# Key-value sums built transposed in two-part features, with K's maxima as a bias of the exponentials and five weight blocks streamed through one buffer

## The chip, the cores and the metric

The kernel runs on one core of one Trainium2 chip. The metric is the device time of one execution in microseconds. A core has five engines that work at the same time and meet through semaphores: TensorE (PE, matmuls; its weight loads are shown as PEld), VectorE (DVE), ScalarE (ACT), GpSimd (POOL) and SyncE (SP), whose queue issues all DMA transfers of this kernel. Each engine works through its own instructions in order. Matmuls write to PSUM (8 banks of 128 x 512 float32), everything else lives in SBUF or, outside the core, in DRAM.

## The reference

For 8 batches and 8 heads of 576 rows and 64 columns, a linear attention with an exponential feature map is computed, and then a mixer with a low-rank token step and a two-layer channel step.

```python
def phi(x):
    proj = np.einsum('bhsd,df->bhsf', x, w_phi)            # d_feat = 128
    proj = proj - np.max(np.abs(proj), axis=-1, keepdims=True)
    return np.concatenate([np.exp(proj), np.exp(-proj)], axis=-1)
q_p, k_p = (phi(q), phi(k))
kv = np.einsum('bhsf,bhsd->bhfd', k_p, v)
z = np.sum(k_p, axis=2)
num = np.einsum('bhsf,bhfd->bhsd', q_p, kv)
den = np.einsum('bhsf,bhf->bhs', q_p, z)[..., None] + 1e-06
attn = num / den            # then heads side by side: x of 8 x 576 x 512
xt = x.transpose(0, 2, 1)
u = x + (xt @ U @ V).transpose(0, 2, 1)                    # rank 32 over the 576 rows
out = u + np.maximum(u @ w_ch1, 0.0) @ w_ch2               # 512 -> 2048 -> 512
```

So every feature vector of K and Q has 256 entries: the exponential of the shifted projection, and the exponential of its negative, where the shift is the largest absolute value of the row. w_ch1, w_ch2, U and V arrive as float64.

## The kernel before

**Attention.** The work unit is a pair of heads of one batch (class Pair; 32 pairs). Of the 576 rows, 512 are the main part (NT = 4 tiles of 128 rows) and 64 are the tail; the tails of both heads are worked on together. A pair goes through eight steps: s_project_k0, s_project_k1, s_project_q0, transposes (of the pair that comes next), s_kv0_q1, s_kv1, s_out0, s_out1. The main loop has the current pair cur at its outputs while the next pair nxt is projected and summed, and a third one, far, is loaded. project_k makes the projections of K for one head, k_features takes the row maxima (L348), subtracts them (L350) and makes both halves of the features with two exponentials over all four tiles (L353, L354). kv_tail and kv_main (L436, L443) multiply the features (f32, 128 x 128, stationary) with V (f32, 65 columns, moving) into one PSUM bank; the 65th column of V is all ones, so that it gives z. kv_done copies the bank to SBUF (L449), and out_tail and out_main (L469, L482) multiply Q's features with it; normalize divides.

**Two parts.** Float32 operands are multiplied in two ways. Tiles typed F32 go to PE as they are. Elsewhere a value is split into a high part, rounded to the type F32R, and a low part, the rest; products of these parts are accumulated. From batch 2 on (self.split, SPLIT = 2, 24 pairs) the projections of K and Q work in two parts, on data that was transposed by 32 x 32 blocks on DVE (L315) after a DMA that reads with 128-byte runs (L265).

**Mixer.** One group of 512 rows (class Mixer; nine groups: eight batches, and one made of all tails) goes through 16 blocks f of the hidden layer. hidden(f) makes 12 matmuls of 512 columns into ph (L619; one PSUM bank of its own), ACT and DVE take the rectified high and low parts out (L624, L625), and add(f) makes 12 matmuls into four banks o (L640). The order of a group's chunks is hidden(0), hidden(1), add(0), hidden(2), add(1) and so on. The chunks of a batch's group are dealt out over the steps of the next batch's attention, 28 of 32 over 34 steps, by Pace.step: after each attention step comes one chunk, or none.

**Weights.** w_ch1 and w_ch2 come as float64 words, are made float32 by convert on ACT, DVE and POOL, and split in two parts during the first batches, while mixer group 0 runs. All 16 blocks stay in SBUF (pool home, tags w1_f and w2_f) but for two: blocks 0 and 8 are stored to DRAM (kept) once, and from group 1 on they take turns in block 0's buffer (STREAM, function stream, L204): when the last matmul that reads one of them is issued, the load of the other is issued. Blocks 8 and 15 are kept in a buffer for both matrices at once (WHOLE); that of block 8 (w_late) later holds y, the group's rows that come in transposed (L605, L611).

**Order.** The program is written in one order, and a planner, which simulates the engines' times, arranges each engine's instructions from it; the order on each engine is then fixed. The PSUM banks are 3 of tag at (attention and token step), 1 of tag ph and 4 of tag o. Where tokens() and the mixer's first rows come at the end of a batch, the next pair's last four steps are dealt in between.

Of the kernel before, what the change touches and what calls it, by code (L numbers as in the profile page):

```python
# [21 lines left out]
P = 128  # L22
# [3 lines left out]
def tile_kernel(  # L26
# [160 lines left out]
    WHOLE = {LAST: "w_last", 8: "w_late"}  # L187
    STREAM = (0, 8)
    kept = {f: dram.tile([P, 2, 2, C], F32, name=f"kept{f}") for f in STREAM}

    def place(f, dt, shape, name):

        if f in WHOLE:
            both = home.tile([P, 2, *shape], dt, tag=WHOLE[f], name=name)
            return both[:, 0], both[:, 1]
        return [home.tile([P, *shape], dt, tag=f"w{n}_{f}", name=f"{name}_{n}") for n in (1, 2)]

    def stream(n, g, f):

        to = STREAM[1 - STREAM.index(f)]  # L200
        if g == 0 or g == B and to == 0:
            return
        w = home.tile([P, 2, C], F32R, tag=f"w{n + 1}_0", name=f"w{n + 1}_{to}_{g}")
        nc.sync.dma_start(out=f32(w), in_=kept[to][:, n])  # L204
        (w1_t, w2_t)[n][to] = w
# [9 lines left out]
    def convert_block(i):  # L215
        f, n = divmod(i, 2)
        r = convert(words[f][n], f"w{n + 1}_{f}")
        if f not in WHOLE:
            w = home.tile([P, 2, C], F32R, tag=f"w{n + 1}_{f}", name=f"w{n + 1}_{f}")
            split_w((nc.scalar.copy, nc.vector.tensor_copy)[n], r, w)  # L220
        elif n == 0:
            found[f] = r
            return
        else:
            w1_w, w = place(f, F32R, (2, C), f"w_{f}")
            split_w(nc.scalar.copy, found[f], w1_w)
            split_w(nc.vector.tensor_copy, r, w)
            w1_t[f] = w1_w
# [20 lines left out]
    class Pair:  # L249
# [93 lines left out]

        def k_features(self, n, k_w, kp):
# [4 lines left out]
                out=mk, in_=k_w, axis=AX.X, op=ALU.max, apply_absolute_value=True)  # L349
            nc.vector.tensor_tensor(  # L350
# [40 lines left out]
        def project_k_split(self, g):  # L391
# [13 lines left out]
            return self.k_features(g, k_w, kp)  # L405
# [26 lines left out]
        def kv_tail(self):  # L432
            self.kv_ps = self.ps("kv_ps", True)
            self.kv_v = self.kv_ps[:, 0:4 * (D + 1)].rearrange("p (f h e) -> p f h e", f=2, h=2)
            for f in range(2):
                nc.tensor.matmul(  # L436
                    self.kv_v[:, f, :, :], self.kpt[:, 0, f * F:(f + 1) * F], self.vt,
                    start=(f == 0), stop=False, skip_group_check=True)
# [59 lines left out]
        def s_project_k1(self):  # L498
            self.kp1 = self.project_k(1)
            self.project_q_tail()  # L500

        def s_project_q0(self):
            self.qp0 = self.project_q(0)

        def s_kv0_q1(self):
            self.kv_tail()
# [3 lines left out]
        def s_kv1(self):  # L510
            self.kv_main(1, self.kp1)
# [318 lines left out]
    if True:  # L830
# [17 lines left out]
        for n, (b, j) in enumerate(pairs):  # L848

            far = Pair(*pairs[n + 2]) if n + 2 < len(pairs) else None  # L850
# [84 lines left out]
```

## Time and profile before

| | |
|---|---|
| time, median of 3 runs | 1227.1 us (1226.07 to 1227.72) |
| the profiled execution: time, span | 1233.19 us, 1231.4 us |
| mean granted clock of TensorE | 0.992 |
| busy: PE, DVE, ACT, POOL | 1204.2, 690.9, 538.2, 203.6 us |
| DMA: bytes moved, mean busy share of q1 | 100.60 MB, 31.2% |

The span runs from the first to the last instruction of the profiled execution; a little of its time lies outside it. The busy time of an engine is the union of its instructions' times. Line numbers are those of the kernel before. A row of the groups gives line, engine, operation, the tile written and those read, shapes, the count, then busy time, the mean duration of one in ns, and the idle time of the engine ahead of them with what ended it. A row of a timeline gives the start, the time taken and what ran, with a count where equal ones follow each other. Durations of matmuls overlap, since they are pipelined.

### The profile page before, as it was taken

The numbers are of one execution on the slowest core, as the hardware profiler recorded it, in microseconds if no ns is written. First come the engines' busy times: TensorE is split into PE (matmuls) and PEld (weight loads), VectorE is DVE, ScalarE is ACT, GpSimd is POOL, SyncE is SP. The second block draws the span as 40 slices with busy tenths as digits, with TensorE's granted clock in tenths as the row PEclk, the third lists the DMA queues.
The fourth block names the chain that finished last, engine by engine and source line by source line (L and its number), as shares of the span: only waits on it lengthen the run. The fifth ranks groups of instructions, "written<-read, shape, count | busy, mean of one in ns | idle before, by whom it ended". The sixth has DMA issues, their size and how long they took to land.

```text
span 1231.4 us, 18285 instructions
## 1 busy us (share of the span) xinstructions
PE 1204.2 (98%) x6667; PEld 1036.6 (84%) x6669; DVE 690.9 (56%) x1517; ACT 538.2 (44%) x1151; POOL 203.6 (17%) x154
## 2 busy tenths in 40 slices
PE   8999998999999999999999999999999999999997
PEld 7887787888888888888888888888888888888886
DVE  5857879775566656665647556655656543312111
ACT  6866678554543444444534444344434431111110
POOL 3533444211110111011111111011201110000000
PEclk9979999999999999999999999999999999999999
DMA  4766221331234213431244123421343015400201
GB/s 133 241 227 208 70 64 30 90 109 25 54 97 116 48 40 91 90 99 30 64 115 111 28 52 86 111 69 26 88 107 98 1 52 150 112 35 1 69 1 35
DMA packets 248345, 100.60 MB, mean 82 GB/s; under 512 B 215360, under 2 KB 227904, under 8 KB 248256
## 3 DMA queue, kind: packets, MB, share of 16 engines
q1 hardware_dynamic: 248256, 99.44, 31.2%
q8 instruction: 53, 0.87, 0.3%
q14 instruction: 36, 0.29, 0.1%
HBM read 78.41 MB, written 20.97 MB: 81 GB/s over the span
## 4 chain that ended last, share of the span: by engine, by line
PE 78%; DVE 8%; SPq 4%; ACT 4%; DMA 4%; issue 1%; POOL 0%; DVEq 0%; ACTq 0%; POOLq 0%
PE ph L619 27%; PE o L640 27%; PE kv_ps L443 7%; PE xp L482 7%; SPq L605 2%; SPq L265 2%; PE pk L399 2%; DVE w L236 1%; PE pp L561 1%; PE kv_ps L436 1%; PE pq L422 1%; DMA raw<-in_q_dram 1%; PE pq L423 1%; PE xpt L469 1%; DMA y<-u_dram 1%
## 5 line engine op out<-in xcount | busy, mean ns | idle before, releaser
L619 PE MATMUL ph<-uT_hi,w 128*128 128x512 f32 x1152 | 389.0, 395 | 4.7 <-DVE h_lo L625 3.3
L640 PE MATMUL o<-w,h_hi 128*128 128x512 f32 x1152 | 327.1, 395 | 3.2 <-ACT h_hi L624 3.2
L619 PEld LDWEIGHTS ph<-uT_hi,w 128*128 128x128 f32 x1152 | 216.2, 188 | 51.2 <-DVE h_lo L625 5.6
L640 PEld LDWEIGHTS o<-w,h_hi 128*128 128x128 f32 x1152 | 211.1, 188 | 45.3 <-ACT h_hi L624 4.9
L619 PE MATMUL ph<-uT_lo,w 128*128 128x512 f32 x576 | 225.1, 391 | 0.0
L624 ACT ACTIVATE h_hi<-ph 128x512 fp32r<-128x512 f32 x144 | 85.9, 596 | 272.0 <-PE ph L619 261.0
L625 DVE SCALAR_TENSOR_TENSOR h_lo<-ph,h_hi 128x512 fp32r<-128x512 f32 x144 | 98.6, 685 | 176.6 <-ACT h_hi L624 175.4
L640 PE MATMUL o<-w,h_lo 128*128 128x512 f32 x576 | 191.9, 395 | 0.6 <-DVE h_lo L625 0.6
L363 POOL PARTITION_ALL_REDUCE qp<-qp x64 | 126.7, 1980 | 286.6 <-ACT qp L362 268.1
L443 PEld LDWEIGHTS kv_ps<-vb,kp 128*128 128x128 f32 x1024 | 126.6, 195 | 2.8
L482 PEld LDWEIGHTS xp<-kv,qp 128*128 128x128 f32 x1024 | 124.1, 194 | 4.8 <-DVE kp L403 0.9
L619 PEld LDWEIGHTS ph<-uT_lo,w 128*128 128x128 f32 x576 | 108.3, 188 | 21.3 <-DVE uT_lo L244 0.6
L443 PE MATMUL kv_ps<-vb,kp 128*128 128x65 f32 x1024 | 126.0, 274 | 0.1
L482 PE MATMUL xp<-kv,qp 128*128 128x65 f32 x1024 | 124.0, 274 | 0.6 <-DVE kp L403 0.6
L640 PEld LDWEIGHTS o<-w,h_lo 128*128 128x128 f32 x576 | 105.4, 188 | 21.6 <-DVE h_lo L625 1.3
L353 ACT ACTIVATE kp<-kp 128x512 f32<-128x512 f32 x64 | 40.4, 632 | 132.9 <-DVE kp L350 83.4
L363 POOL PARTITION_ALL_REDUCE qp_t<-qp_t x32 | 27.2, 851 | 403.2 <-ACT qp_t L362 401.0
L319 DVE TENSOR_TENSOR T<-raw,T 64x512 fp32r<-64x512 f32 x96 | 68.5, 714 | 33.6 <-ACT T L318 31.1
L315 DVE STREAM_TRANSPOSE raw<-raw 128x512 f32<-128x512 f32 x48 | 34.1, 711 | 80.3 <-DMA raw<-in_q_dram 36.8
L318 ACT CAST T<-raw 64x512 fp32r<-64x512 f32 x96 | 59.3, 618 | 33.9 <-PE pq L423 23.4
L365 ACT ACTIVATE qp<-qp 128x512 f32<-128x512 f32 x64 | 40.4, 631 | 59.8 <-DVE qp L364 59.5
L146 POOL INT64_ADD w_ab<-w_ab x32 | 44.1, 1377 | 76.0 <-DVE w_ab L142 40.4
(128 smaller groups left out, 1357.1 us busy)
## 6 DMA issues: line engine op xcount, KB each, us to landing
words<-in_moe_w_ch_dram SPq DMA_DIRECT2D x32, 512.0 KB, 8.0
w<-kept SPq DMA_DIRECT2D x30, 512.0 KB, 4.1
vb<-in_v_dram SPq DMA_DIRECT2D x64, 128.0 KB, 2.5
u_dram<-x SPq DMA_DIRECT2D x32, 256.0 KB, 2.2
st<-u_dram SPq DMA_DIRECT2D x16, 512.0 KB, 4.0
out_dram<-st SPq DMA_DIRECT2D x32, 256.0 KB, 2.3
y<-u_dram SPq DMA_DIRECT2D x112, 64.0 KB, 2.4
raw<-in_k_dram SPq DMA_DIRECT2D x192, 32.0 KB, 2.0
```

The source lines that it names most:

```text
L146: nc.gpsimd.int64_add(a64, a64, b64)
L318: nc.scalar.copy(out=m[here, s, :], in_=x_[here])
L319: nc.vector.tensor_sub(m[there, s, :], x_[here], f32(m[here, s, :]))
L353: nc.scalar.activation(out=kp[:, :, 0:F], in_=kp[:, :, F:2 * F], func=AF.Exp)
L363: nc.gpsimd.partition_all_reduce(qp[:, 0, :], qp[:, 1, :], P, ReduceOp.absmax)
L365: nc.scalar.activation(out=qp[:, 0, :], in_=qp[:, 1, :], func=AF.Exp)
L443: nc.tensor.matmul(self.kv_v[:, f, g, :], kp[:, t, f * F:(f + 1) * F], self.vb[:, g, t, :], start=False, stop=(t == NT - 1), skip_group_ch ...
L482: nc.tensor.matmul(xv[:, c, :], qp[:, f, c * P:(c + 1) * P], self.kv[:, f, c // 2 if self.split else s, :], start=(f == 0), stop=(f == 1))
L619: nc.tensor.matmul(ph, w1_part(f, l, c), r[:, c, :], start=(n == 0), stop=(n == 3 * NCC - 1))
L624: on_act = nc.scalar.activation(out=h_hi, in_=ph, func=AF.Relu)
L625: on_dve = nc.vector.scalar_tensor_tensor(out=h_lo, in0=ph, scalar=0.0, in1=f32(h_hi), op0=ALU.max, op1=ALU.subtract)
L640: nc.tensor.matmul(self.o[t], l[:, cs], w2_t[f][:, r, :], start=(f == 0 and n == 0), stop=(f == NFC - 1 and n == 2))
```

## The change

All of it is for the 24 pairs of batches 2 to 7, but for the weights' homes.

- The sums over the rows are built transposed. v_parts splits V in two parts that lie side by side (v_hl, 128 columns: 64 high, 64 low) and serve as the stationary operand; k_parts splits K's features in two parts (khi, klo), which move, 256 columns each. kv_turned makes 4 tiles x 2 parts = 8 matmuls a head in F32R, and the upper and lower half of the result are added to kvT (features in the free dimension). kv_end, called at the start of the iteration in which the pair is cur, turns kvT back with two f32 transposes, has kv_tail's matmuls in front of the sum, and adds the parts into kv.
- z of the main rows no longer comes from a column of ones: k_sums adds up the four tiles on DVE, sums over partitions on POOL, and takes one row to DRAM (zd); k_sums_turned reads it back with features in the partitions (zc).
- k_features no longer subtracts the maxima: they are made negative (less) and go to ACT as the bias of the exponentials, one 128-column exponential for each tile and sign. The tails' features go the same way.
- Blocks 0, 3, 6, 9 and 12 now take turns in block 0's buffer. The homes of 3, 6 and 9 get the tags late0 to late5, which hold the new tiles from batch 2 on: khi of head 0 in late0, of head 1 in late5, klo of both heads in late1, zs in late2, v_hl in late3, kvT in late4. Block 12 takes block 8's place in w_late, and block 8 gets a home of its own.

```diff
-    WHOLE = {LAST: "w_last", 8: "w_late"}
-    STREAM = (0, 8)
+    WHOLE = {LAST: "w_last", 12: "w_late"}
+    STREAM = (0, 3, 6, 9, 12)
...
+    def place_of(n, f):
+        if f in STREAM[1:]:
+            return f"late{2 * STREAM.index(f) - 2 + n}"
+        return f"w{n + 1}_{f}"
...
-        to = STREAM[1 - STREAM.index(f)]
+        to = STREAM[(STREAM.index(f) + 1) % len(STREAM)]
...
+        def k_sums(self, g, kp):
+            if g == 0:
+                self.zs = home.tile([P, 2, 2, 2 * F], F32, tag="late2", name=f"zs{self.nm}")
+                self.zd = dram.tile([2, 2 * F], F32, tag="zd", bufs=2, name=f"zd{self.nm}")
+            zs = self.zs[:, g]
+            nc.vector.tensor_add(zs, kp[:, 0:2, :], kp[:, 2:4, :])
+            nc.vector.tensor_add(zs[:, 0, :], zs[:, 0, :], zs[:, 1, :])
+            nc.gpsimd.partition_all_reduce(zs[:, 1, :], zs[:, 0, :], P, ReduceOp.add)
+            nc.sync.dma_start(out=self.zd[g:g + 1, :], in_=zs[0:1, 1, :])
+
+        def k_sums_turned(self):
+            self.zc = small.tile([P, 2, 2], F32, tag="zc", bufs=2, name=f"zc{self.nm}")
+            nc.sync.dma_start(
+                out=self.zc.rearrange("p g n -> p (g n)"),
+                in_=self.zd.rearrange("g (n f) -> f (g n)", f=F))
+
+        def k_parts(self, g, kp):
+            hi = home.tile([P, NT, 2 * F], F32R, tag=f"late{5 * g}", name=f"khi{self.nm}_{g}")
+            lo = home.tile([P, NT, 2 * F], F32R, tag="late1", name=f"klo{self.nm}_{g}")
+            nc.scalar.copy(out=hi, in_=kp)
+            nc.vector.tensor_sub(lo, kp, f32(hi))
+            return hi, lo
+
+        def v_parts(self):
+            self.v_hl = home.tile([P, 2, NT, 2 * D], F32R, tag="late3", name=f"v_hl{self.nm}")
+            src = self.vb[:, :, :, 0:D]
+            nc.scalar.copy(out=self.v_hl[:, :, :, 0:D], in_=src)
+            nc.vector.tensor_sub(
+                self.v_hl[:, :, :, D:2 * D], src, f32(self.v_hl[:, :, :, 0:D]))
+
+        def kv_turned(self, g, parts):
+            kt = self.kt = self.ps(f"kt{g}_")
+            for t in range(NT):
+                for n in range(2):
+                    nc.tensor.matmul(
+                        kt[:, 0:2 * F], self.v_hl[:, g, t, :], parts[n][:, t, :],
+                        start=(t == 0 and n == 0), stop=(t == NT - 1 and n == 1))
+            if g == 0:
+                self.kvT = home.tile([P, 2, 2 * F], F32, tag="late4", name=f"kvT{self.nm}")
+            r_ = slice(g * D, (g + 1) * D)
+            nc.scalar.copy(out=self.kvT[r_, 1, :], in_=kt[D:2 * D, 0:2 * F])
+            nc.vector.tensor_add(self.kvT[r_, 0, :], kt[0:D, 0:2 * F], self.kvT[r_, 1, :])
+
+        def kv_end(self):
+            if not self.split:
+                return
+            kb = self.kt[:, 2 * F:4 * F]
+            for f in range(2):
+                nc.tensor.transpose(
+                    out=kb[:, f * P:(f + 1) * P], in_=self.kvT[:, 0, f * F:(f + 1) * F],
+                    identity=ident)
+            self.kv_tail()
+            self.kv = small.tile([P, 2, 2, D + 1], F32, tag="kv", bufs=1, name=f"kv{self.nm}")
+            nc.vector.tensor_copy(out=self.kv, in_=self.kv_v)
+            nc.vector.tensor_add(
+                self.kv[:, :, :, 0:D], self.kv[:, :, :, 0:D],
+                kb.rearrange("p (f h d) -> p f h d", f=2, h=2))
+            nc.vector.tensor_add(
+                self.kv[:, :, :, D:D + 1], self.kv[:, :, :, D:D + 1],
+                self.zc.rearrange("p g n -> p n g").unsqueeze(3))
+
         def k_features(self, n, k_w, kp):
...
+            if self.split:
+                less = small.tile([P, 16], F32, tag="less", name=f"less{self.nm}_{n}")[:, 0:ng]
+                nc.vector.tensor_scalar(
+                    out=less, in0=mk, scalar1=-1.0, scalar2=None, op0=ALU.mult)
+                for t in range(ng):
+                    for i, (scale, by) in enumerate(((1.0, less), (-1.0, mk))):
+                        nc.scalar.activation(
+                            out=kp[:, t, i * F:(i + 1) * F], in_=k_w[:, t, :], func=AF.Exp,
+                            scale=scale, bias=by[:, t:t + 1])
+                return kp
...
-            return self.k_features(g, k_w, kp)
+            self.k_features(g, k_w, kp)
+            self.k_sums(g, kp)
+            return kp
...
         def s_project_k1(self):
             self.kp1 = self.project_k(1)
             self.project_q_tail()
+            if self.split:
+                self.v_parts()

         def s_project_q0(self):
             self.qp0 = self.project_q(0)
+            if self.split:
+                self.parts0 = self.k_parts(0, self.kp0)

         def s_kv0_q1(self):
+            if self.split:
+                self.k_sums_turned()
+                self.kv_turned(0, self.parts0)
+                self.qp1 = self.project_q(1)
+                self.parts1 = self.k_parts(1, self.kp1)
+                return
...
         def s_kv1(self):
+            if self.split:
+                self.kv_turned(1, self.parts1)
+                return
...
         for n, (b, j) in enumerate(pairs):
+            cur.kv_end()
```

More of the change, by code (lines that the diff above doesn't have):

```diff
@@ L195, in place @@
             return both[:, 0], both[:, 1]
-        return [home.tile([P, *shape], dt, tag=f"w{n}_{f}", name=f"{name}_{n}") for n in (1, 2)]
+        return [home.tile([P, *shape], dt, tag=place_of(n, f), name=f"{name}_{n}") for n in (0, 1)]
     def stream(n, g, f):
-        to = STREAM[1 - STREAM.index(f)]
+        to = STREAM[(STREAM.index(f) + 1) % len(STREAM)]
         if g == 0 or g == B and to == 0:
@@ L218, in convert_block @@
         if f not in WHOLE:
-            w = home.tile([P, 2, C], F32R, tag=f"w{n + 1}_{f}", name=f"w{n + 1}_{f}")
+            w = home.tile([P, 2, C], F32R, tag=place_of(n, f), name=f"w{n + 1}_{f}")
             split_w((nc.scalar.copy, nc.vector.tensor_copy)[n], r, w)
@@ L437, in kv_tail @@
                     self.kv_v[:, f, :, :], self.kpt[:, 0, f * F:(f + 1) * F], self.vt,
-                    start=(f == 0), stop=False, skip_group_check=True)
+                    start=(f == 0), stop=self.split and f == 1, skip_group_check=True)
         def kv_main(self, g, kp):
```

## The prediction

> **What bounds the kernel now.** I read the page's totals and chain first, then the stage in which the changed pairs run, then single stretches. The page:
>
> ```profile
> span 1231.4 us, 18285 instructions
> ...
> PE 1204.2 (98%) x6667; PEld 1036.6 (84%) x6669; DVE 690.9 (56%) x1517; ACT 538.2 (44%) x1151; POOL 203.6 (17%) x154
> ...
> PE 78%; DVE 8%; SPq 4%; ACT 4%; DMA 4%; issue 1%; POOL 0%; DVEq 0%; ACTq 0%; POOLq 0%
> ```
>
> TensorE is busy 98% of the span and has 78% of the chain. The change touches only pairs of batches 2 to 7, so I cut the middle of the run into its cycles of one batch (four pairs and one mixer group), and took one short stretch where two batches meet. Columns: stretch, its length, PE, PEld, DVE, ACT, POOL busy, clock, DMA.
>
> ```profile
> 527.40:662.10 134.70, 133.85 (x768) 116.38 (x767) 80.59 (x183) 59.55 (x132) 18.93 (x12) 1.00 0.33 76
> 662.10:796.90 134.80, 133.85 (x768) 116.28 (x766) 79.81 (x182) 59.62 (x132) 18.95 (x12) 1.00 0.32 74
> ...
> 648.00:664.00 16.00, 15.34 (x88) 13.14 (x86) 15.18 (x34) 7.58 (x16) 0.74 (x1) 1.00 0.40 85
> ```
>
> A cycle lasts 134.8 us, 33.7 a pair; PE lacks 0.95 us of it, DVE works 79.8 (59%), ACT 59.6 (44%). So here a microsecond off PE is a microsecond off the run, as long as the others keep up. The last row is the weak place: where the tokens of a batch meet the next pairs, DVE is busy 15.18 of 16 us, and nearly all of PE's waiting in the whole stage lies there:
>
> ```profile
> PE o L640 <- ACT h_hi L624: 1.3, 3, 0.7
> PE o L640 <- DVE h_lo L625: 0.6, 1, 0.6
> PE ph L619 <- DVE h_lo L625: 0.2, 1, 0.2
> ```
>
> That is 2.1 us of waiting from 259 to 1000 us.
>
> **What PE saves.** The durations of matmuls overlap, so I price them from start to next start, in PE's timeline of one pair:
>
> ```profile
> 694.14 0.63 PE L561 MATMUL pp<-xs,u_all 128*128 128x256 f32 x4
> 694.62 1.09 PE L640 MATMUL o<-w,h_lo 128*128 128x512 f32 x4
> ...
> 701.41 1.90 PE L443 MATMUL kv_ps<-vb,kp 128*128 128x65 f32 x16
> 703.11 0.48 PE L422 MATMUL pq<-T,w_hl 128*128 128x512 f32 x1
> 703.43 0.39 PE L423 MATMUL pq<-T,w_hl 128*128 128x512 f32 x1
> 703.66 1.09 PE L640 MATMUL o<-w,h_lo 128*128 128x512 f32 x4
> 704.58 1.89 PE L443 MATMUL kv_ps<-vb,kp 128*128 128x65 f32 x16
> 706.28 0.48 PE L619 MATMUL ph<-uT_hi,w 128*128 128x512 f32 x1
> 706.60 0.39 PE L619 MATMUL ph<-uT_lo,w 128*128 128x512 f32 x1
> ```
>
> kv_main calls 8 matmuls a head, and the trace shows 16: an f32 matmul is two passes of about 0.106 us, and a head takes 703.11 - 701.41 = 1.70 us. A 512-column matmul right behind f32 work takes 0.32 us (703.11 to 703.43) where the next takes 0.23: a change of type costs 0.09. Old cost a pair: 2 x (1.70 + 0.09) = 3.58 us.
>
> The new kv_turned calls 8 matmuls a head of exactly the form of L561 (fp32r, 128x128 stationary, 256 columns), which take (694.62 - 694.14)/4 = 0.12 us and appear once each: 2 x 8 x 0.12 = 1.92 us. kv_end adds two f32 transposes; kv_tail moves there unchanged, and that f32 group is now followed by its own change of type, 0.09. The transposes' price by the group of L593 below is at most 5.0/32 = 0.16 each, and at least nothing; I take 0.125 (nearer the row), 0.25 in all. Net: 3.58 - 1.92 - 0.25 - 0.09 = 1.32 us a pair.
>
> ```profile
> L443 PE MATMUL kv_ps<-vb,kp 128*128 128x65 f32 x1024 | 126.0, 274 | 0.1
> L363 POOL PARTITION_ALL_REDUCE qp<-qp x64 | 126.7, 1980 | 286.6 <-ACT qp L362 268.1 <-PE ph L619 18.5
> L353 ACT ACTIVATE kp<-kp 128x512 f32<-128x512 f32 x64 | 40.4, 632 | 132.9 <-DVE kp L350 83.4 <-DVE den_t L456 34.7 <-DVE den L456 14.3
> L403 DVE TENSOR_TENSOR kp<-pk,kp 128x256 f32<-128x256 f32 x96 | 37.4, 409 | 2.0 <-ACT kp L402 2.0
> L399 PE MATMUL pk<-w_hl,T 128*128 128x256 f32 x192 | 34.9, 286 | 0.0
> L402 ACT COPY kp<-pk 128x256 f32<-128x256 f32 x96 | 33.3, 371 | 35.0 <-PE pk L399 34.8
> L350 DVE TENSOR_TENSOR kp<-kp,mk 128x512 f32<-128x512 f32 x48 | 33.1, 690 | 1.2
> L243 ACT CAST uT_hi<-y 128x512 fp32r<-128x512 f32 x28 | 15.7, 612 | 9.9 <-PE ph L619 9.8 <-DVE y L611 0.2
> L353 ACT ACTIVATE kp_t<-kp_t 128x128 f32<-128x128 f32 x32 | 9.9, 310 | 21.1 <-DVE kp_t L350 20.8
> L456 DVE TENSOR_SCALAR den<-xp 128x4 f32<-128x4 f32 x64 | 10.2, 160 | 27.9 <-PE xp L482 27.2
> L593 PE MATMUL pt<-ident,x 128*128 128x128 f32 x32 | 5.0, 279 | 1.3 <-DVE x L578 0.6 <-DVE st L659 0.5 <-DVE uT_lo L244 0.2
> ```
>
> L399 runs only in changed pairs, 8 times each: 192/8 = 24 pairs. **PE's gain is 24 x 1.32 = 31.7 us**; with transposes at 0 to 0.16 and the matmul at 0.115 to 0.13 it is 24 to 40.
>
> A rule on this: the Trainium skill (TensorE: Matmul & The Clock Gate, Back-to-back issue gap) gives 256 columns as N/2.4 + 2.5, 109 ns. By it the gain would be 16 x 0.011 x 24 = 4 us larger; L561's 120 ns is of this very form, so the row decides.
>
> **What the other engines get, for one pair.** ACT: out go 4 exponentials of 512 columns (4 x 0.632 = 2.53). In come 16 of 128 columns with a bias (by L353's kp_t, 0.310: 4.96), two copies of 1024 columns (L243's 512 take 0.612 and L402's 256 take 0.371, so 0.24 per 256 columns, and 0.612 + 2 x 0.24 = 1.09 each; 2.19), one of 512 (0.61) and two of 64x256 from PSUM (0.37, 0.74). Net +6.0 us, from 14.9 to 20.9 of 33 us. DVE: out go two subtractions of 512 columns and the tail's small one (2 x 0.69 + at most 0.41, say 1.7). In come three tiny negations (3 x 0.16 = 0.48), sums for z (2 x (0.69 + 0.41) = 2.20), two subtractions of 1024 columns (0.69 + 2 x 0.28 = 1.25 each, 2.50), one of 512 (0.69), two kvT additions (0.82), two additions in kv_end (0.41 + 0.16 = 0.57). Net +5.6 us, from 20.0 to 25.6, 78% of the new period. POOL: two all-reduces of 128x256, each under the 1.98 us of L363's 512 columns: at most 4 us on top of 4.7. None of these is at its limit over a cycle, so PE hides them, except in the crowded stretch.
>
> There, one tail, two project_k steps and one kv_end fall into 16 us in which DVE has 0.8 us left. They bring 0.48 + 2.20 + 0.69 + 0.57 - 1.7 = 2.2 us net. So DVE is late by about 2.2 - 0.8 = 1.4 us there, what is late next is h_lo L625, and PE waits for it. With six such meetings that is 8.4 us; the bounds are 0 (DVE's work slides into the lighter stretches on either side) and 6 x 3.9 = 23 (nothing that goes out falls into the stretch).
>
> Another rule speaks against the exponentials: the Trainium skill (ScalarE: Activation LUTs, What ACT_TABLE_LOAD costs) says that a per-partition bias operand adds about 93 ns to an activation. No run here has shown such an operand yet; by it ACT gets 16 x 0.093 = 1.5 us a pair more, and if that fell on the path in each crowded stretch the sum would end at 1213 instead. ACT is busy only 7.58 of 16 us there, so I leave it out of the sum.
>
> **Waits and queues.** The K chain is longer: maximum, negation, 8 exponentials (2.5 us instead of 1.3), then sums, the copy (1.09) and klo (1.25). For head 0 two steps lie before kv_turned(0). For head 1 klo shares its buffer with head 0's, so it starts only when kv_turned(0) is through: at least 1.25 us plus hand-over, beside 0.55 us of project_q and mostly one mixer chunk (12 matmuls, 2.7 us). I take nothing; without the chunk it costs 0.7 us a pair. After kv_turned(1) there are now two hops (copy 0.37, add 0.41; transposes; copy and two adds 1.0) where one copy stood, with a chunk behind each. Taken as hidden; 1 us a pair if a chunk is missing.
>
> ```profile
> w<-kept SPq DMA_DIRECT2D x30, 512.0 KB, 4.1
> u_dram<-x SPq DMA_DIRECT2D x32, 256.0 KB, 2.2
> raw<-in_k_dram SPq DMA_DIRECT2D x192, 32.0 KB, 2.0
> ```
>
> Streaming grows from 30 loads to 8 x 2 x 4 + 7 x 2 = 78, and six more stores to kept. Each load starts when its predecessor's last reader is through and is needed three feature blocks later, with at least four chunks (10.8 us) between: 4.1 us is hidden twice over; the 48 extra are 197 us of landing time spread over 980 us with DMA at a third. The homes that the streamed blocks leave (3, 6, 9) are read for the last time in batch 0's mixer group, before the first changed pair's sums, features and kvT go there, and w_late (now block 12) before y needs it in batch 2: no wait. Three small DMAs a pair go to SP's queue. zd waits for POOL's all-reduce, zc for zd's landing (2 us, as u_dram); zc's 512 four-byte pieces have no row, 2.0 us by raw's nearest, and kv_end needs them some 8 us later. What is queued behind them is the raw loads, and behind those DVE's transposes.
>
> **Sum.** The profiled execution took 1233.2 us (span 1231.4 and 1.8 around it), 6.1 more than the median of 1227.1. 1233.2 - 31.7 + 8.4 = 1209.9; less 6.1, the forecast is **1204 us**, own range 1194 to 1216.
>
> **Rivals.**
> *All hidden* (15%): DVE's extra in the crowded stretch slides away: 1227.1 - 31.7 = 1195. For it: 41% idle DVE over a cycle. Against: PE already waits there.
>
> *Kv's hand-over* (13%): klo's shared buffer and the second hop each keep PE waiting in most pairs, 0.7 + 0.3 us: 24 more, 1228, or 1216 if half of the pairs are hit. For it: steps without a chunk (28 chunks on 34 steps). Against: PE's order can put other chunks there.
>
> *DVE's queue decides, slower* (17%): what DVE stands still for, in order, in 259 to 1000 us:
>
> ```profile
> DVE h_lo L625 <- ACT h_hi L624: 44.1, 37, 3.7
> DVE T L319 <- ACT T L318: 31.1, 16, 3.0
> DVE raw L315 <- DMA raw<-in_q_dram: 30.5, 19, 2.9
> DVE raw L315 <- DMA raw<-in_k_dram: 30.2, 17, 3.8
> ```
>
> DVE's idle time is 33.7 - 20.0 = 13.7 us a pair, and each wait at the head of its queue holds all behind it, h_lo too. With 25.6 us of work and 32.4 of new period, 6.8 us may stay; beyond that DVE sets the pace. If 9 stay (raw later behind zc, h_hi later behind 16 exponentials), a pair takes 34.6 us: 24 x 0.9 = +22, 1249. Against: these waits are where DVE had nothing else due, and shrink when it is late.
>
> *No gain on PE* (5%): the f32 passes cost less than their records say. Then 1227 + 8 = 1236. Against: the following matmul really starts 1.70 us later.
>
> **Numbers.** 50% is the forecast's. A measurement here tells 0.2% from no change. Faster: 50 + 15 + 10 of the hand-over's 13 = 75%; same 5%; slower 20%. The range 1192 to 1236 leaves out most of the DVE rival and little below.
>
> **What would show it.** Right: fp32r kv matmuls at 0.12 us, once each; cycles of about 131 us; PE waits of 1 to 2 us more per cycle, at the meetings, ended by h_lo. Wrong: PE waiting for klo, kvT or kv in every pair, DVE near 90% through the cycles, or w L204 late at L619.

## The result, and the profile after

The changed kernel takes 1268.2 us (median of four runs, 1263.9 to 1274.4), the kernel before on the same chip 1226.6: a ratio of 1.032, 95% interval 1.029 to 1.035. It is slower by 42 us, where I forecast 23 us faster, and outside the range. The profiled execution took 1270.6 us. The page after, totals and chain:

```profile
span 1268.8 us, 18691 instructions
...
PE 1208.0 (95%) x6331; PEld 1021.5 (81%) x6333; DVE 821.8 (65%) x1781; ACT 680.0 (54%) x1559; POOL 314.9 (25%) x202
...
PE 66%; DVE 14%; SPq 6%; ACT 6%; DMA 5%; issue 2%; POOL 1%; DVEq 0%; ACTq 0%; POOLq 0%
```

The view of the cores:

```profile
core 0: 1268.8 us, clock 0.968
```

PE has 336 instructions fewer, and yet it is busy 3.8 us longer. The two views together give an account of the 37.4 us by which the span grew. PE's idle time went from 1231.4 - 1204.2 = 27.2 to 1268.8 - 1208.0 = 60.8 us: **+33.6**. The granted clock went from 0.992 to 0.968; the missing share times the span is 9.9 us before and 40.6 after: **+30.7** of slower work. What is left, 37.4 - 33.6 - 30.7 = **-26.9**, is work that PE no longer has, where I had 31.7. (The share counts PE's idle time at half clock too, so 30.7 and 26.9 are upper bounds; going by the time that PE was busy at half clock, 71.1 us after and 17.1 before, they are 27 and 23.) So PE's saving came, and more than twice as much went in two new places: PE stands, and PE runs at half clock.

Neither shows at first sight in the cycles. The windows after, columns as in the prediction:

```profile
401.40:536.50 135.10, 133.12 (x693) 112.80 (x692) 96.63 (x217) 81.84 (x196) 38.42 (x20) 0.95 0.38 91
536.50:673.70 137.20, 131.34 (x712) 111.21 (x711) 106.74 (x229) 82.63 (x200) 38.56 (x20) 0.99 0.39 96
673.70:812.40 138.70, 131.81 (x706) 112.93 (x707) 101.51 (x225) 83.12 (x201) 37.51 (x20) 0.97 0.38 95
```

A cycle takes 135 to 139 us, not the 131 I had written, though DVE works only 97 to 107 us of it (about 74%; I had 78%), ACT 82 to 83 and POOL 38. PE's longest waits from 260 to 1040 us (sum, times, longest):

```profile
PE pk L480 <- DVE kv L408: 3.9, 2, 2.2
PE pk L480 <- DVE kv L407: 3.6, 2, 3.0
PE ph L715 <- ACT uT_hi L249: 3.4, 3, 1.5
PE ph L715 <- DVE uT_lo L250: 2.8, 5, 1.0
PE xp L565 <- DVE den_t L539: 2.6, 2, 1.5
...
PE kt L387 <- DVE klo L372: 0.2, 1, 0.2
```

Many small waits of different kinds, and klo, which I had feared, has hardly a part in them. Five batches (from the first matmul of group 1's hidden(0) to that of group 6's, 20 of the 24 changed pairs) lose 21.8 us in gaps, where the kernel before loses 2.2, and spend 47.8 us at half clock, where it spends none. PE is busy in 41.9 of these 47.8, so about 21 us of work are added by the clock. In these batches the account is 19.6 us more idle time and 21 us of slower work, less 22 us of saved work: 18.6 us longer (672.3 before, 690.9 after). Of the other 18.8 us by which the span grew, 4.6 lie ahead of these batches and 14.2 behind them; they were not followed.

**Where they lie.** All but 3 of the 21.8 us gather where a batch ends. The rows of x of the finished batch go to u_dram, come back as y, are turned and split, and only then can the next group's hidden(0) begin. The kernel before, timeline of DVE (the last rows of x, and the last part of the next group's input), and below it PE's:

```profile
640.01 0.66 DVE L578 TENSOR_TENSOR xt<-xt,vp 64x512 f32<-64x512 f32 x1
...
655.72 0.68 DVE L244 TENSOR_TENSOR uT_lo<-y,uT_hi 128x512 fp32r<-128x512 f32 x1
```

```profile
656.48 1.07 PE L640 MATMUL o<-w,h_lo 128*128 128x512 f32 x4
657.38 0.39 PE L619 MATMUL ph<-uT_hi,w 128*128 128x512 f32 x1
```

The way takes 15.7 us, and PE fills it with chunks of the old group, the last of which ends when the new input is there, within a microsecond. After, DVE and then PE at the same place:

```profile
666.73 0.66 DVE L674 TENSOR_TENSOR xt<-xt,vp 64x512 f32<-64x512 f32 x1
...
681.20 0.68 DVE L250 TENSOR_TENSOR uT_lo<-y,uT_hi 128x512 fp32r<-128x512 f32 x1
```

```profile
667.95 1.15 PE L736 MATMUL o<-w,h_lo 128*128 128x512 f32 x4
...
671.94 0.51 PE L480 MATMUL pk<-w_hl,T 128*128 128x256 f32 x2 [2.17 <-DVE kv L408]
...
673.67 0.50 PE L715 MATMUL ph<-uT_hi,w 128*128 128x512 f32 x1 [0.68 <-ACT uT_hi L249]
675.70 3.68 PE L565 MATMUL xp<-kv,qp 128*128 128x65 f32 x16 [1.53 <-DVE den_t L539]
```

The way is about as long as before (14.5 us), but the old group's last matmuls end at 669.1, 1.7 us after x. Then PE has only the pair's own steps and waits for each of them, and from 674.4 it runs at half clock (16 f32 matmuls of 65 columns take 3.68 us instead of 1.89).

The old group's chunks are gone because they ran earlier. To count them, I take the windows from the first matmul of the group's hidden(0) to the last of pp (the token step's first product, ahead of x), with ph's and then o's matmuls alone; a chunk is 12. Before:

```profile
522.70:624.40 101.70, 36.61 (x144) 26.28 (x144) 8.26 (x12) 7.16 (x12) 1.00 0.29 70
522.70:624.40 101.70, 34.34 (x133) 23.72 (x132) 2.56 (x4) 1.00 0.29 70
```

After:

```profile
536.50:651.80 115.30, 44.63 (x168) 31.16 (x168) 8.86 (x13) 8.34 (x14) 0.99 0.37 91
536.50:651.80 115.30, 41.81 (x156) 28.34 (x157) 1.33 (x2) 0.99 0.37 91
```

(144 + 133)/12 = 23 of 32 chunks before, (168 + 156)/12 = 27 after. The same reading as a mean over five meetings, in us, from the same rows of the two timelines; the last two columns are what the experiments below moved:

| kernel | last pp to x | x to uT_lo | old chunks run on after x | chunks done at the last pp |
|---|---|---|---|---|
| before | 15.7 | 16.0 | 16.9 | 23.0 |
| after | 11.3 | 16.0 | 1.0 | 28.7 |

### The profile page after: what moved, and what is told of

The parts are those of the page before. It is cut to its first block, busy times and chain, and to the rows that moved or that the text cites. A ratio compares the mean times of both kernels' runs of the same rounds, so it can differ in the third digit from the quotient of the medians.

```text
span 1268.8 us, 18691 instructions
## 1 busy us (share of the span) xinstructions
PE 1208.0 (95%) x6331; PEld 1021.5 (81%) x6333; DVE 821.8 (65%) x1781; ACT 680.0 (54%) x1559; POOL 314.9 (25%) x202
## 3 DMA queue, kind: packets, MB, share of 16 engines
q1 hardware_dynamic: 268800, 127.86, 37.4%
## 4 chain that ended last, share of the span: by engine, by line
PE 66%; DVE 14%; SPq 6%; ACT 6%; DMA 5%; issue 2%; POOL 1%; DVEq 0%; ACTq 0%; POOLq 0%
PE o L736 24%; PE ph L715 23%; PE xp L565 7%; SPq L701 4%; PE kt L387 3%; SPq L271 2%; DVE T L325 2%; DVE w L242 2%; DMA u_dram<-x 1%; PE pk L480 1%; DMA y<-u_dram 1%; PE pp L657 1%; DVE x L674 1%; PE kv_ps L526 1%; PE kv_ps L519 1%
## 5 line engine op out<-in xcount | busy, mean ns | idle before, releaser
L736 PE MATMUL o<-w,h_hi 128*128 128x512 f32 x1152 | 314.0, 398 | 5.9 <-ACT h_hi L720 4.0
L358 POOL PARTITION_ALL_REDUCE zs<-zs x48 | 107.7, 2243 | 356.4 <-DVE zs L357 342.3
L736 PE MATMUL o<-w,h_lo 128*128 128x512 f32 x576 | 181.9, 395 | 2.7 <-DVE h_lo L721 2.6
L444 POOL PARTITION_ALL_REDUCE qp<-qp x64 | 131.6, 2057 | 186.3 <-ACT qp L443 186.3
L565 PEld LDWEIGHTS xp<-kv,qp 128*128 128x128 f32 x1024 | 131.1, 204 | 7.6 <-DVE den_t L539 3.1
L565 PE MATMUL xp<-kv,qp 128*128 128x65 f32 x1024 | 132.6, 285 | 3.0 <-DVE den_t L539 2.6
L715 PEld LDWEIGHTS ph<-uT_lo,w 128*128 128x128 f32 x576 | 110.5, 192 | 26.9 <-DVE uT_lo L250 6.3
L325 DVE TENSOR_TENSOR T<-raw,T 64x512 fp32r<-64x512 f32 x96 | 78.3, 816 | 21.2 <-ACT T L324 18.5
L427 ACT ACTIVATE kp<-kp,less 128x128 f32<-128x128 f32 x192 | 61.5, 391 | 54.3 <-DVE less L423 49.4
L427 ACT ACTIVATE kp<-kp,mk 128x128 f32<-128x128 f32 x192 | 63.6, 390 | 0.1
L372 DVE TENSOR_TENSOR klo<-kp,khi 128x1024 fp32r<-128x1024 f32 x48 | 63.0, 1312 | 0.8 <-ACT khi L371 0.6
```

The lines of the kernel that those rows point to most:

```text
L325: nc.vector.tensor_sub(m[there, s, :], x_[here], f32(m[here, s, :]))
L358: nc.gpsimd.partition_all_reduce(zs[:, 1, :], zs[:, 0, :], P, ReduceOp.add)
L372: nc.vector.tensor_sub(lo, kp, f32(hi))
L427: nc.scalar.activation(out=kp[:, t, i * F:(i + 1) * F], in_=k_w[:, t, :], func=AF.Exp, scale=scale, bias=by[:, t:t + 1])
L444: nc.gpsimd.partition_all_reduce(qp[:, 0, :], qp[:, 1, :], P, ReduceOp.absmax)
L565: nc.tensor.matmul(xv[:, c, :], qp[:, f, c * P:(c + 1) * P], self.kv[:, f, c // 2 if self.split else s, :], start=(f == 0), stop=(f == 1))
```

## The experiments

Of each kernel's runs the median and the ratio to the kernel before, with its interval, are given. "Cover" is the column "old chunks run on after x" of the table above, again as a mean over five meetings. The runs were made on several chips; differences in us between kernels of different chips are worked out from the ratios.

**1. PE's saving alone.** Is a microsecond off PE really one off the run? The kernel before, with 6 of 16 f32 matmuls of each changed pair left out, nothing added:

```diff
             for t in range(NT):
-                for f in range(2):
+                for f in range(1 if self.split and t < 3 else 2):
```

> The kernel before with 3 of 4 matmuls of the second feature half of kv left out in the 24 pairs (kv is then wrong in that half): 6 f32 matmuls or 12 passes of 0.106 us, 1.3 us a pair, as much as the change saves on TensorE, and nothing is added anywhere. If TensorE's time is worth what the prediction took it for: 1190 to 1205 us. If the pairs' chain of before has no room (the other engines and buffers already set the pace): 1215 or more.

1204.8 us, 0.979 (0.976 to 0.982): 25.8 us of the 24 x 12 x 0.106 = 30.5 taken off PE. A cycle of it:

```profile
512.20:642.80 130.60, 128.75 (x720) 111.35 (x719) 80.67 (x184) 60.00 (x133) 20.13 (x13) 1.00 0.33 77
```

That is the cycle of 131 us that I had forecast, at full clock, with cover 16.7. The missing 4.7 us are waits: in the five batches PE is busy 25.4 us less, its gaps grow from 2.2 to 6.6, and the time falls by 21.0. The first term of the sum stands; the loss is in what the change adds. (PE less busy does not by itself upset the order.)

**2. Streaming alone, and the bias alone**, each put into the kernel before:

```diff
-    WHOLE = {LAST: "w_last", 8: "w_late"}
-    STREAM = (0, 8)
+    WHOLE = {LAST: "w_last", 12: "w_late"}
+    STREAM = (0, 3, 6, 9, 12)
...
```

> The kernel before with the five streamed weight blocks alone. Theory (the work added on VectorE and ScalarE makes the attention chain of each pair longer than TensorE's work, so the mixer's matmuls run out before a batch ends): 1223 to 1232 us, no change, since TensorE's and the other engines' work is the same. Rival (the 48 more loads and SyncE's queue hold up the raw loads): at least 10 us of the 41 are here, 1237 or more.

1237.4 us, 1.0077 (1.0052 to 1.0101): 9.5 us, which I had priced at nothing, in the prediction and here, and by its time at the lower edge of what I had given the rival. Gaps over the five batches are 5.8 us instead of 2.2, at full clock; the rest of the loss lies outside these batches and was not followed.

```diff
+            if self.split:
+                less = ...            # minus the maxima
+                for t in range(ng):   # exponentials of 128 columns with a bias
```

> The kernel before with the maxima as a bias of 128-column exponentials alone. It takes 1.2 us a pair from VectorE and adds about 3.9 us a pair to ScalarE (16 exponentials of 0.39 us against 4 of 0.63). Theory: ScalarE stays near 60% and VectorE is eased, so 1222 to 1234 us. Rival (the 16 small exponentials and the longer way to K's features are what delays the pairs): 1240 or more.

1231.0 us, 0.9997 (0.9976 to 1.0018): no change that can be measured. And the other way round, the change with the old subtraction:

```diff
-            if self.split:
-                less = ...            # the bias exponentials, left out again
```

> The changed kernel with the subtraction and the two 512-column exponentials of before in place of the bias. VectorE gets 1.2 us a pair more, ScalarE 4 us less. Theory, if VectorE is the bound: the same or slower, 1268 to 1285 us; if ScalarE's length of the chain counts: 1235 to 1255.

1267.6 us, 1.028 (1.024 to 1.032): the intervals overlap with the whole change's. The bias is neither cause nor cure.

**3. z's way.** k_sums and k_sums_turned left out, with POOL's reduction and three DMAs a pair; zc is a constant, so the denominators are not the reference's.

```diff
         def k_sums(self, g, kp):
-            ...
+            pass
         def k_sums_turned(self):
-            ...
+            self.zc = zc_fixed       # memset to 300 once
```

> The changed kernel without z of the main rows: no sums on VectorE, no all-reduce on GpSimd, no zd and zc transfers; a constant stands in for z, so the output's denominators are not the reference's. It takes 2.2 us a pair from VectorE, 4.5 from GpSimd and three waiting transfers from SyncE's queue. Theory: VectorE's work falls from 24 to 22 us a pair, and the time by a good part of what was lost, to 1225 to 1245 us. Rival (kv's second hop, PSUM banks held until kv is added up, and ScalarE): 1255 or more.

1269.5 us, 1.031 (1.028 to 1.035): nothing gained. A cycle:

```profile
530.30:672.30 142.00, 138.72 (x729) 119.23 (x730) 94.05 (x218) 85.67 (x210) 20.27 (x12) 0.94 0.40 100
```

DVE has 94 us of work in 142, fewer than after, and still no time comes back. This speaks against the rival that DVE's queue sets the pace by its amount of work, and against z's hops as the cause. What is left to be late is the way of kv, or the order.

**4. The order: chunks held back.** Of a group's 32 chunks HELD are not dealt over the steps. Were the chunks only dealt too early, more of them held back would cover the meeting again.

```diff
-    HELD = 4
+    HELD = 8        # and 12; in the kernel before 8
```

> The changed kernel with HELD = 8 instead of 4: eight of a group's 32 chunks are kept back until the tokens of the next batch are done, so 24 are dealt over the 34 steps. Theory (in the changed kernel 27 to 32 chunks are used up when the token step's last pp matmul runs, where it was 23 before, so nothing covers the way from x over u_dram to y, TensorE stands, and then runs at half clock): the waits at the meetings shrink, the granted clock rises above 0.98, and the time falls to 1205 to 1240 us. Rival (the chain of the pairs through the other engines is simply longer): 1260 or more.

1270.0 us, 1.032 (1.026 to 1.037).

> The changed kernel with HELD = 12. Theory: as with 8 or better, 1200 to 1240 us; chunks that are held too long could pile up ahead of the next group. Rival: 1260 or more.

1263.8 us, 1.027 (1.024 to 1.031).

> The kernel before with HELD = 8. TensorE has no waits to lose at the meetings there, so theory: 1223 to 1236 us, no gain. If it gains over 10 us, the setting and not the change explains the difference.

1239.3 us, 1.007 (1.005 to 1.010).

> The changed kernel without z of the main rows (a constant stands in for it, the denominators are not the reference's) and with HELD = 8. If the other engines' added work matters once the chunks are there, it is faster than HELD = 8 alone by 5 us or more; if TensorE is the bound again, within 5 us of it.

1263.5 us, 1.027 (1.023 to 1.031), with z left out as in 3.

The cover became 1.4 us with 8 and 3.1 with 12, of the 16 needed. The planner arranges PE's order itself and took the chunks forward all the same, so in the changed kernel this edit hardly moved what it was to move, and says little on the cause. In the kernel before the same edit did move it, from 16.9 to 41.8 us, and cost 0.7%: there the planner left the chunks back. Leaving out z as well gave 6 us, but the intervals overlap.

**5. The order: chunks pinned.** So the first matmul of each chunk was held at its place in the written order.

```diff
-                    nc.tensor.matmul(ph, ...)          # and the same in add
+                    ins = nc.tensor.matmul(ph, ...)
+                    if n == 0 and 0 < self.g < B - 1:  # or, for late12 and late10_h8: ... and f >= 12 (10)
+                        tc.keep_in_program_order(ins)
```

> The changed kernel with the first matmul of every mixer chunk of groups 1 to 7 kept in the written order on TensorE, so that 23 of 32 chunks stand ahead of the token step's last pp matmul, as before the change (27 to 30 in the changed kernel). Theory (the planner's early chunks are the loss): no waits at the meetings, clock back to 0.99, 1195 to 1225 us. Rival (the pairs' chain through the other engines is longer than TensorE's work, and the early chunks only filled its waits): the waits appear in the middle of the pairs instead, 1245 us or more.

1298.8 us, 1.055 (1.050 to 1.060).

> All chunks kept in the written order, and z of the main rows left out (a constant stands in, the denominators are not the reference's), which takes 2.2 us a pair from VectorE and 4.5 from GpSimd. If VectorE's added work makes waits once the order is restored, this is faster than the kernel with all chunks kept by 8 us or more; if not, within 5 us of it.

1316.8 us, 1.068 (1.063 to 1.072), with z left out as in 3.

> The changed kernel with only the chunks of blocks 12 to 15 kept in the written order (24 to 25 chunks ahead of the last pp matmul). Theory: most of the waits at the meetings go, 1205 to 1235 us; rival: 1245 or more.

1294.9 us, 1.051 (1.048 to 1.054).

> The changed kernel with the chunks of blocks 10 to 15 kept in the written order and HELD = 8 (22.8 chunks ahead of the last pp matmul). Theory: waits at the meetings gone while the planner may still fill waits earlier in the batch, 1195 to 1230 us, at or below the kernel with all chunks kept in order; rival: 1245 or more.

1290.4 us, 1.047 (1.045 to 1.050), with HELD = 8 besides.

With all chunks pinned the cover is 24.4 us and 23.0 chunks are done at the last pp, where it was 16.9 and 23.0 before the change: the chunks again reach past the whole way from x to uT_lo, which takes 21.1 us here. And the kernel is 28 us slower still. A cycle, and PE's waits from 260 to 1060 us:

```profile
557.80:700.30 142.50, 132.47 (x712) 112.15 (x711) 103.83 (x226) 82.24 (x200) 37.21 (x21) 0.99 0.38 93
```

```profile
PE pq L505 <- DVE tail_T L303: 10.6, 5, 2.5
PE pqt L494 <- DVE x L544: 8.6, 10, 1.3
PE kt L387 <- ACT qp L443: 8.0, 5, 1.6
PE pk L480 <- DVE less_t L423: 7.2, 5, 1.8
PE pp L657 <- DVE xs L644: 5.3, 7, 1.1
```

PE's gaps over five batches rose from 21.8 to 51.7 us. Only 16.8 of them lie between the last pp and 5 us behind uT_lo, where in the changed kernel nearly all lay; the others now lie inside the pairs: PE is at a step for which the other engines are not ready, and each row shows a tile of that pair's chain (tails, x, Q's features, K's maxima). So my theory that the early chunks alone are the loss fell; as I read it, the chunks that the planner takes forward fill waits in the pairs that are there anyway. In the written order 51.7/5 = 10 us a batch of waits are left bare, and there is only one supply of chunks to cover them and the meeting. The blocks 12 to 15 alone, or 10 to 15 with HELD = 8, give covers of 22.8 and 41.0 us and are no cure either. And one run fits neither reading: with z left out, so with less work for DVE and POOL, the pinned kernel became 18 us slower, not faster.

**6. Which part makes the pairs late?** First the added work without kt: k_sums, both parts, v_parts, the bias and the streaming stay, but kv is made by kv_main as before, and the new tiles are not used.

```diff
-                self.kv_turned(0, self.parts0)
+                self.kv_tail()
+                self.kv_main(0, self.kp0)
...
-            cur.kv_end()
```

> The changed kernel with kv made by kv_main's f32 matmuls as before, while the sums, the parts of K and V, the bias exponentials, the transfers and the streaming are still done but kv does not use them (z comes from the column of ones). TensorE's work is that of before; VectorE, ScalarE, GpSimd and SyncE carry all but the kvT part of the added work. If that work is the loss: 1260 or more. If the new way of kv itself is (two more PSUM banks a pair, the second hop, kv waiting for the parts): 1232 to 1248, the time of the streaming alone and little more.

1294.7 us, 1.053 (1.050 to 1.056): 55 us over streaming alone, and no PE work was added.

```profile
542.60:687.70 145.10, 139.25 (x766) 119.50 (x766) 100.11 (x211) 80.19 (x193) 37.19 (x21) 0.97 0.38 92
```

```profile
PE o L734 <- ACT h_hi L718: 12.3, 9, 2.1
PE pk L480 <- DVE xt L544: 8.1, 5, 3.5
```

The chunks are not what ran short here: the cover is 16.3 us and 24.8 chunks are done at the last pp, as with streaming alone (17.0 and 24.5). But the way from x to uT_lo takes 19.9 us instead of 15.2, and 11 of the 30.1 us of gaps in the five batches lie away from the meetings. These batches are 45.5 us longer than with streaming alone: 24 in gaps, 15 by the clock, and about 6 that were not accounted for.

This one number would close the account: 1226.6 - 25.8 (experiment 1) + 9.5 (streaming) + 55 = 1265, a ratio of 1.032. But the other half alone does nearly as much. Streaming and the old kv, with kt's bank turns as idle extras: a bank of tag at taken for each head, one matmul into it, the copy and the addition into kvT, two transposes, one addition at the end, all unused:

```diff
+                self.bank_turn(0)    # kt: 1 matmul; ACT copy and DVE add into kvT; again for head 1
...
+            cur.bank_end()           # 2 transposes of kvT into kt's bank, 1 DVE add
```

> The kernel before with the five streamed blocks and, beside its own kv, the bank turns of the change: a bank for each head's kt with one matmul instead of eight, the copy and addition to kvT, and the two transposes and one addition at kv_end, all unused. It adds 0.46 us a pair to TensorE, 11 us in all, and 1.2 us to VectorE. If the third PSUM bank and the two hops are the loss: 1262 or more, with TensorE waiting at the meetings and a lower clock; if not, 1237 + 11, 1243 to 1255.

1296.6 us, 1.054 (1.051 to 1.058); 57 us over streaming alone, of which 24 x (2 x 0.12 + 2 x 0.125) = 12 is its own PE work.

```profile
536.90:686.80 149.90, 146.36 (x781) 125.91 (x781) 84.84 (x195) 62.99 (x141) 19.55 (x12) 0.92 0.35 88
```

```profile
PE ph L651 <- ACT uT_hi L249: 7.4, 8, 1.8
PE ph L651 <- DVE uT_lo L250: 7.0, 10, 1.6
```

Here DVE and ACT are hardly busier than before the change (85 and 63 us a cycle), and the cover is 3.5 us. So either half alone costs some 50 us (55, and 45 without its own PE work) and the two together about 56 (39.6 + 25.8 - 9.5, from the ratios): they do not add.

If kv's hops were the price, fewer should help. kvT is now turned back by matmuls that accumulate into kv_tail's own bank, z by four one-column matmuls on zs, so that one copy makes kv, with no reduction on POOL and no small DMAs:

```diff
-                nc.tensor.transpose(out=kb[...], in_=self.kvT[...], identity=ident)
+                nc.tensor.matmul(self.kv_v[:, f, :, 0:D], self.kvT[...], ident..., start=False, ...)
+                nc.tensor.matmul(self.kv_v[:, f, g, D:D + 1], self.zs[...], ones, ...)   # z
...
-            nc.vector.tensor_add(self.kv[...], self.kv[...], kb...)
-            nc.vector.tensor_add(self.kv[...], self.kv[...], self.zc...)
```

> The changed kernel with kv_end mended: kvT is turned back by f32 matmuls with the identity that add straight into kv_tail's bank, and z is added there too by four one-column matmuls on zs, so kt's bank is free after its two readers, one copy ends kv, and the all-reduces and the zd and zc transfers are gone. If the long hold of kt's bank and the second hop are the loss: 1215 to 1240; if the bank turns as such and the work on the other engines: 1250 or more.

1315.3 us, 1.068 (1.066 to 1.071): worse. The cover is -5.7 us (the old group is through before x is written), and five batches have 94 us at half clock. It also puts f32 matmuls back on PE, which I did not price apart.

**7. Which pairs?** The change for the two middle pairs of a batch, and for the first and last, whose steps lie at the meetings:

```diff
-                self.split ...                             # wherever the change asks for it
+            self.turned = self.split and j in (1, 2)       # or (0, 3)
```

> The changed kernel with the new way of kv (bias, parts, sums, kvT) for the pairs j = 1 and 2 of batches 2 to 7 alone; pairs 0 and 3, whose keys or outputs fall beside the token step and the mixer's new rows, stay as before. TensorE saves 12 x 1.3 = 16 us, streaming costs 8. If the loss sits where two batches meet: 1215 to 1232 us, at or below the kernel before. If the added work costs wherever it is: half of the way from the streaming alone (1237) to the changed kernel (1268), 1245 to 1260.

1266.4 us, 1.029 (1.025 to 1.033).

> The same with the new way for the pairs j = 0 and 3 alone, those beside the meeting. If the loss sits there: 1250 to 1290 us, at least 20 above the kernel with pairs 1 and 2. If the added work costs wherever it is: within 10 us of that one.

1252.9 us, 1.019 (1.015 to 1.024).

Over streaming alone, which all three kernels have, half of the pairs cost 26 us (1, 2) or 14 us (0, 3), and all of them 30; the cover is 4.5 and 11.8 us. I had guessed the opposite order, since the meeting is where the time shows. It shows there whatever pair it comes from: nearly all of the 20.8 and 16.1 us of gaps in the five batches lie there.

No kernel that computes the whole reference came out faster than the one before.

## Why the prediction was wrong

**The step that failed** is "None of these is at its limit over a cycle, so PE hides them, except in the crowded stretch". The shares were right and the conclusion does not follow from them. Over a cycle DVE stands at 74%, and nothing shows it as the bound. i_load gives the other engines the work without changing PE's, DVE stands at 69% there (100.1 of 145.1 us), and the time grows by 55 us over streaming alone: PE did not hide it. How this comes about is in part argued. PE's order is fixed, and work for other engines that is in a pair's chain can make PE's next instruction late even on an engine with a quarter of its time free. Before, the free matter that absorbs this, 32 chunks a batch, was used up: the prediction quoted that PE lacks 0.95 us in 134.8. I read this as "PE bounds, so the others have room". It also says that the chunks just cover what there is to wait for, and at the meeting with 1.15 us to spare: the old group's last matmul ends at 657.55, uT_lo at 656.40. In the changed kernel 28.7 chunks instead of 23.0 are gone before the meeting, so a chunk that fills a new wait in the pairs is missing there. i_load shows that this is not the only way to lose: its chunks are there, but what they have to cover is 4.7 us longer, and there are waits inside the pairs besides. The way of reading that I missed stood in the trace before.

**The term** that stood for this, "Sum"'s +8.4 (lateness of 1.4 us at six meetings; bounds 0 to 23), was looked for at the right place with the wrong mechanism: DVE's busy time in the stretch. In the runs the same term is 55 (i_load) or 45 (h_banks without its own PE work). The upper bound of 23 assumed that at worst the work inside the stretch is late. (By its own terms it is 6 x (3.9 - 0.8) = 19.) In the changed kernel the chunks ran short at the stretch, and they had been used up ahead of it.

**Half clock** was no term at all. It makes 27 to 31 of the 61 to 64 us lost.

**What PE saves** was right as a price of the matmuls. kt's matmuls after, in PE's timeline, first and last of a head and what follows:

```profile
664.36 0.28 PE L387 MATMUL kt<-khi,v_hl 128*128 128x256 f32 x1
...
665.19 0.28 PE L387 MATMUL kt<-klo,v_hl 128*128 128x256 f32 x1
665.31 0.40 PE L673 MATMUL vp<-pst,v_all 128*64 128x512 f32 x1
```

Eight in 0.95 us, 0.119 each, once each. The account above gives 23 to 27 us and experiment 1 gives 25.8 of 30.5, so the 31.7 was some 5 us too much, and the saving lies at the low end of my bounds of 24 to 40 (worked out again, the lower one is 24 x 1.09 = 26); "No gain on PE" is out.

**What the other engines get** was nearly right. The groups after:

```profile
L358 POOL PARTITION_ALL_REDUCE zs<-zs x48 | 107.7, 2243 | 356.4 <-DVE zs L357 342.3 <-DVE den_t L539 11.3 <-PE pp L657 2.8
L427 ACT ACTIVATE kp<-kp,mk 128x128 f32<-128x128 f32 x192 | 63.6, 390 | 0.1
L372 DVE TENSOR_TENSOR klo<-kp,khi 128x1024 fp32r<-128x1024 f32 x48 | 63.0, 1312 | 0.8 <-ACT khi L371 0.6
L371 ACT CAST khi<-kp 128x1024 fp32r<-128x1024 f32 x48 | 50.2, 1046 | 0.4
```

klo 1.31 us (I had 1.25), khi 1.05 (1.09), POOL's sum 2.24 (I had it under 1.98: a sum of 256 columns takes longer than the maximum of 512, which took 1.98 before and 2.06 after). The exponential with a bias takes 0.390 instead of the 0.310 without, 80 ns more. The Trainium skill (ScalarE: Activation LUTs, What ACT_TABLE_LOAD costs), which I cited, states about 93 ns, and the trace comes near it. Experiment 2 shows that this costs no time here.

**Waits and queues.** klo's shared buffer is hidden, as I took it (0.2 us). The second hop is not: L407 and L408 end 7.5 us of PE's longest waits: there a pk cannot start until kv has been read out of its bank. Streaming was taken as hidden and cost 9.5 us.

**The rivals.** The nearest in time was "DVE's queue decides, slower" (1249), whose price was DVE's amount of work; experiment 3 speaks against that. Its remark that a wait at the head of a queue holds all behind it fits the new waits, but I gave it a threshold in idle time. That its sign came out is no merit of its price. "All hidden" is out; "Kv's hand-over" has its mechanism in the trace, with a small part of its price.

**What stays open.** Why either half alone is enough. Three things could carry it: a later order on the in-order queues of DVE and ACT, three banks of tag at held longer (some of PE's waits end when a PSUM tile has been read, as at L407 and L408), or the planner, which arranges everything anew for each kernel and may do it badly. No run tells them apart: each edit moves all three, and g_pin moved the order without mending the time. That the loss does not follow the amount of work speaks for the order, of the queues or the planner: without z's work nothing came back (e4_no_z) or the time grew (g_pin_noz), and two of four pairs cost nearly as much as all (j_12). A kernel with the work and an order made by hand would be the test; none was run.

## What to carry to other kernels

Where PE is full because filler work covers every wait, ask how much filler is left at the tightest place; a busy share of 60% on the other engines is no answer. Price added work on the chain that PE's next instruction waits for, even on an engine with time to spare, and measure it alone (added but unused, beside the old path) before the saving is built. And when pauses begin to appear on PE, count the clock with them: here it about doubled the loss.

## What the runs showed of the hardware

The clock was halved after short pauses. Windows of 3.4 us after, at the meeting shown above:

```profile
667.60:671.00 3.40, 2.17 (x15) 1.80 (x13) 3.37 (x8) 0.37 (x1) 0.00 (x0) 1.00 0.59 114
671.00:674.40 3.40, 1.55 (x7) 1.00 (x7) 1.97 (x6) 1.52 (x4) 0.00 (x0) 0.99 0.79 124
674.40:677.80 3.40, 2.10 (x10) 2.10 (x11) 3.17 (x8) 0.81 (x2) 0.00 (x0) 0.50 0.77 120
677.80:681.20 3.40, 3.40 (x14) 3.11 (x14) 3.16 (x12) 3.30 (x11) 0.00 (x0) 0.50 0.70 242
681.20:684.60 3.40, 3.40 (x24) 3.07 (x23) 3.40 (x7) 3.18 (x8) 1.30 (x1) 1.00 0.68 167
```

The three waits in PE's timeline are 2.17, 0.68 and 1.53 us, 4.4 us in about 6, and none is as long as a window. The third began only 0.2 us before the clock fell, so it fell behind the first two; PE was busy 64% and 46% of the two windows ahead. The clock fell to 0.50 for 6.8 us, the second half of which PE worked through without a pause. Over five batches this added about 21 us of work (half of the 41.9 us in which PE was busy at half clock), as much as the gaps themselves (21.8). Not every short pause did it: i_less has one of 1.70 us, up to 640.0, and keeps the clock at 1.00 through all five batches. The Trainium skill (TensorE: Matmul & The Clock Gate, A second HAM failure mode: psum-queue depth-cycling) tells of frequent short pauses that make the clock go back and forth, and this trace agrees, with a fall to 0.50 behind pauses of 2.17 and 0.68 us. Its practical rule of no pause over about 3 us (Why this matters for your kernels) would not have warned at this meeting, where no wait is over 2.2.
